# Layer 3 of a four-layer kernel: the weights become the stationary operand, 512 tokens move, and VectorE turns the result

## The chip, the core and the metric

The kernel runs on one core of a Trainium2 chip. The metric is the device time of one execution in microseconds (us), the median of several runs. The engines in this text are TensorE (PE in the profile; PEld is its weight load), VectorE (DVE), ScalarE (ACT), GpSimd (POOL), and SyncE (SP), whose queue issues the DMAs.

## The reference, cut to what matters

```python
def _attn_ref(q, k, v):            # 8 batches, 8 heads, 576 tokens, 64 wide
    q_s = softmax(q, axis=-1); k_s = softmax(k, axis=2)
    kv = np.einsum('bhsd,bhse->bhde', k_s, v)
    return np.einsum('bhsd,bhde->bhse', q_s, kv)
...
x = attn_out.transpose(0, 2, 1, 3).reshape(4608, 512)
h = x @ moe_w_in                   # layer 0: 512 -> 2048
g = np.maximum(0.01 * h, h)
x = g @ moe_w_out                  # layer 1: 2048 -> 512
h = x @ moe2_w_in                  # layer 2: 512 -> 2048
g = h * (1.0 / (1.0 + np.exp(-h)))
return g @ moe2_w_out              # layer 3: 2048 -> 512, the output [4608, 512]
```

The weights arrive as 64-bit floats; the kernel decodes them to 32 bits on ACT and DVE.

## The kernel before, in words

**Precision.** Every fp32 matrix is held as a sum of two float32r parts, high and low, in one tile `[128, 2, 512]`. A product takes three matmuls: high by high, high by low, low by high. ACT copies the high part (line 302), DVE subtracts it from the value to get the low part (line 298).

**Seven products for eight.** Layers 1 to 3 multiply matrices of 2x2 blocks with seven products (c = 1 to 7) in place of eight, with sums of blocks before and sums of products after. The sums of blocks of the weights are made once (`convert`, with a table `PLANS`) and kept in DRAM (`wc`). Of the activations four blocks or sums are kept in DRAM (`gda` for layer 1, `x2d` for layer 2, `gd` for layer 3); three sums more are made on DVE when they are loaded (line 894, `add`).

**Tokens.** 4608 tokens are nine blocks of 512 (`TB`). Layers 1 and 2 go over *supers*: four pairs of blocks and the single last block. Their matmuls have the weights stationary (`lhsT`) and half-blocks of tokens moving: 512 columns for a pair (256 of each block), 256 for the last super. Layer 3 goes over the nine blocks one by one, and there the activations are stationary and the weights move, 256 columns at a time (line 1153): 9 blocks x 4 steps i x 7 products x 12 matmuls = 3024. Its result has tokens in the partitions, so that a finished tile of 512 columns is stored straight from SBUF (`store`, line 1172, 36 stores of 256 KB). Layer 1 in the form of *supers* (line 962) works in two passes over its inner dimension, products 1, 6, 7, 4 (`FIRST`) and then 2, 5, 3 (`SECOND`), with both token halves of a super in PSUM at once: 4 supers x 336 matmuls of 512 columns, and 336 of 256.

**What sets the order.** A planner written in Python (`Queues`) plays all tasks against assumed durations (`v_tt`, `a_`, `pe` and so on for an operation of n columns; 0.73 us for the issue of a DMA of 256 KB and 3 us until it has landed) and ranks, and writes the instructions down in that order. On the chip each engine runs its list strictly in that order, and so does SP's list of DMAs. Operand tiles come from 15 buffers (`g`, `xs`, `xv`, `xr`, `x_108` to `x_115`); a load into one waits until the matmuls that read it are done. 16 tiles `o` of `[128, 512]` hold sums and results. PSUM's eight banks are named `h` and `b`. `a` are weight tiles. Layer 3's weights take the tiles of layer 2's as those come free.

In the code, `layer3` issues the matmuls, `blocks` adds the products of a block up (ACT one copy, DVE eight adds), `store` writes out; `g3_all` loads the operands. `layer1` and `blocks1` are the same for layer 1 (two copies on ACT and six adds on DVE for a token half).

Of the kernel before, what the change touches and what calls it, by code (L numbers as in the profile page):

```python
# [26 lines left out]
def v_tt(n):  # L27
    return 0.16 + n / 960


def v_ts(n):
    return 0.16 + n / 1920


def a_(n):
    return 0.19 + n / 1200


def g_tt(n):
    return 0.15 + n / 430  # L40


def pe(n):
    return 0.007 + n / 2330
# [158 lines left out]
def linear_attention_two_mlps(  # L203
# [62 lines left out]
    gd = [tc.dram_tile([NG, 4, len(s), P, 2, HB], F32, name=f"gd{n}") for n, s in enumerate(supers)]  # L266
# [89 lines left out]
    def split1(f):  # L356
# [336 lines left out]
    def act(j, f, h):  # L693
# [29 lines left out]
    KEPT = (1, 2, 4, 5)  # L723
# [140 lines left out]
    def g1_all():  # L864
        for n in range(NJ):
            pm = merge[n]
            for g, (cs, kind) in enumerate(((FIRST, "b"), (SECOND, ""))):
                for i in range(NG):
                    for q_ in range(2 // pm):
                        at = at1[n, g, i, q_] - 4  # L870
                        yield rank(at)
                        fs = range(4 * i + 2 * q_, 4 * i + 2 * q_ + 2 * pm)
                        yield wait(*(("gd1", j, f) for j in supers[n] for f in fs))
                        src = {
                            c: gd1[n][i, q_ * pm:(q_ + 1) * pm, m].rearrange("z p j n -> p z (j n)")
                            for m, c in enumerate(KEPT1)
                        }
                        yield from operand(
                            [("x", 1, n, g, i, q_)], kind, at, cs, [src], lend, home=HOMES[g]
                        )  # L880

    def g3_all():
        for j in range(NB):
            n, jj = divmod(j, 2)
            for i in range(NG):
                r = at3[j, i] - 4
                yield rank(r)
                yield wait(*(("gd", n, i, rq, c) for c in KEPT for rq in range(2 // merge[n])))
                srcs = {c: gd[n][i, m, jj].rearrange("p r n -> p (r n)") for m, c in enumerate(KEPT)}
                yield from operand([("x", 3, j, i)], "a", r, (1, 5, 2, 6, 4, 7, 3), [srcs], lend)  # L890
# [7 lines left out]
    def blocks(key, r, give):  # L898

        def product(c):  # L900
            yield wait(("p", *key, c))
            return banks[key, c]

        def end(c):
            r_b.put(banks.pop((key, c)))

        p = yield from product(1)
        s = yield get(r_o)
        yield op(("A", a_(TB)))
        copy("A", s, p)  # L910
        end(1)
        p = yield from product(2)
        t = yield get(r_o)
        yield from add(t, s, p)
        end(2)
        spawn(r, give(1, 1, t))
        p = yield from product(6)
        yield from add(s, s, p)
        end(6)
        p = yield from product(7)  # L920
        u = yield get(r_o)
        yield from add(u, s, p)
        end(7)
        p = yield from product(5)
        t = yield get(r_o)
        yield from add(t, u, p)
        spawn(r, give(2, 2, t))
        yield from add(s, s, p)
        end(5)
        p = yield from product(3)  # L930
        yield from add(s, s, p)
        end(3)
        spawn(r, give(1, 2, s))
        p = yield from product(4)
        yield from add(u, u, p)
        end(4)
        spawn(r, give(2, 1, u))

    def layer1():
        for n in range(NJ):  # L940
            w_, pm = width[n], merge[n]
            key = 1, n
            for g, cs in enumerate((FIRST, SECOND)):
                for i, q_ in itertools.product(range(NG), range(2 // pm)):
                    begin, last = not (i or q_), i == NG - 1 and q_ == 2 // pm - 1
                    for c in cs:
                        yield rank(at1[n, g, i, q_])
                        if begin:
                            for mb in range(2 // pm):
                                if c == 2:  # L950
                                    yield wait(("kept", n, mb))
# [3 lines left out]
                        yield wait(("op", ("w", 1, i), c), ("op", ("x", 1, n, g, i, q_), c))  # L955
                        w, x = slot[("w", 1, i), c], slot[("x", 1, n, g, i, q_), c]
# [13 lines left out]
                        if n == NJ - 1 and q_ == 2 // pm - 1:  # L970
                            done(("p", 1, i, c))
                        if last:
                            for mb in range(2 // pm):
                                done(("p", 1, n, mb, c))
                                if c == FIRST[0]:
                                    spawn(-100, blocks1(n, mb))

    def blocks1(n, m):
        key = 1, n

        def product(c):
            yield wait(("p", 1, n, m, c))
# [12 lines left out]
        done(("kept", n, m))  # L995
# [11 lines left out]
        spawn(-100, store1(n, m, 1, 0, t))  # L1007
# [6 lines left out]
        spawn(-100, store1(n, m, 0, 0, t))  # L1014
        p = yield from product(5)
        yield from add(u, u, p)
        spawn(-100, store1(n, m, 1, 1, u))
# [5 lines left out]
        spawn(-100, store1(n, m, 0, 1, s))  # L1023
# [82 lines left out]
    def active(n, i, rq, a, b, t, bank=None):  # L1106
# [6 lines left out]
        if (a, b) == (2, 2):  # L1113
            made["22", n, i, rq] = t
            done(("22", n, i, rq))
            return
        if (a, b) == (1, 2):
            yield wait(("22", n, i, rq))
            t22 = made["22", n, i, rq]
            yield from add(t, t, t22)  # L1120
            spawn(at, keep(n, i, rq, 4, t22))
        yield from keep(n, i, rq, {(1, 1): 1, (2, 1): 2, (1, 2): 5}[a, b], t)

    def keep(n, i, rq, c, t):
        to = gd[n][i, KEPT.index(c)]
        yield op(("D", 0.73))
        nc.sync.dma_start(
            out=to[0] if merge[n] == 2 else to[:, :, rq].rearrange("j p n -> p j n"),
            in_=t.rearrange("p (j n) -> p j n", n=HB),
        )  # L1130
        yield wait()
# [3 lines left out]
    def layer3():  # L1135


        for j in range(NB):
            for i in range(NG):
                for c in ORDER:  # L1140
                    yield rank(at3[j, i])
                    if i == 0:
                        banks[(3, j), c] = yield get(r_b)
                    bank = banks[(3, j), c]
                    yield wait(("op", ("w", 3, i), c), ("op", ("x", 3, j, i), c))
                    x, s = slot[("w", 3, i), c], slot[("x", 3, j, i), c]
                    yield op(("P", 12 * pe(HB)))
                    for m in range(2):
                        for n, (r, a, b) in enumerate(
                            (r, a, b) for r in range(2) for a, b in ((0, 0), (0, 1), (1, 0))  # L1150
                        ):
                            at = r * HB + m * P
                            nc.tensor.matmul(  # L1153
                                bank[:, m * HB:(m + 1) * HB], lhsT=s[:, a, at:at + P],
                                rhs=x[:, b, r * HB:(r + 1) * HB],
                                start=i + m + n == 0, stop=i == NG - 1 and m + n == 6,
                            )
                    r_x.put(s)
                    if i == NG - 1:
                        done(("p", 3, j, c))  # L1160
                        if c == ORDER[0]:
                            spawn(-100, blocks((3, j), -100, lambda a, b, t, j=j: store(j, a, b, t)))

    def layers():
        yield from layer1()
        yield from layer2()
        yield from layer3()

    def store(j, a, b, t):
        o = out[j * TB:(j + 1) * TB, :].rearrange("(p c) e -> p c e", c=4)  # L1170
        yield op(("D", 0.73))
        nc.sync.dma_start(
            out=o[:, 2 * a - 2:2 * a, (b - 1) * HB:b * HB], in_=t.rearrange("p (c e) -> p c e", c=2)
        )
        yield wait()
        r_o.put(t)

    def later():

        yield wait(*(("unit", n) for n in range(len(units))))  # L1180
        r_x.add(*gbuf)
# [23 lines left out]
    for j in range(NB):  # L1205
        for i in range(NG):
            at3[j, i] = t_
            t_ += 2
# [4 lines left out]
    def weight_rank(l, i, c):  # L1213
        if l == 1:
            return at1[0, int(c in SECOND), i, 0] - 8
        return (at2[0, i] if l == 2 else at3[0, i]) - 8

    with tc.manual_schedule():
# [37 lines left out]
        spawn(base[1] - 4, g1_all())  # L1256
        spawn(sum_rank(0, 0), presums())
        spawn(base[2] - 5, x_all())
        spawn(base[3] - 4, g3_all())
# [32 lines left out]
```

## Time and profile before

| | us |
|---|---|
| timed runs (three) | 1574.66, 1574.81, 1577.5; median 1574.81 |
| profiled execution, its own time | 1576.41 |
| profiled execution, span from first to last instruction | 1574.6 |
| PE busy | 1543.8 (98%) |
| DVE busy | 1092.3 (69%) |
| ACT busy | 893.9 (57%) |

Some 1.8 us of the profiled execution's time lie outside its span. Busy times are sums over instructions: where two instructions of an engine overlap in the records, both count. A weight load (PEld) runs beside the matmul ahead of it.

### The profile page before, as it was taken

To read this page: it belongs to the slowest core of one execution; us is meant where nothing else is said; L and a number is where in the kernel's file an instruction comes from. 1 tells how busy PE (TensorE), PEld (TensorE's weight loads), DVE (VectorE), ACT (ScalarE), POOL (GpSimd) and SP (SyncE) were. 2 spreads that over 40 slices of the span, in tenths; PEclk is the share of its full clock that TensorE was granted. 3 is DMA by queue.
4 is the path that set the end of the run, shared out by engine and by line. 5 is a ranking of instruction groups with operands and counts; after the bars stand their busy time and mean duration, and the time that the engine had idled before them with its cause. 6 is when DMAs were issued, how large, how long until landed. Compare 5 with 4: busy or idle time off the path is not lost.

```text
span 1574.6 us, 26644 instructions
## 1 busy us (share of the span) xinstructions
PE 1543.8 (98%) x9088; PEld 1338.1 (85%) x9088; DVE 1092.3 (69%) x2046; ACT 893.9 (57%) x1965; POOL 39.5 (3%) x56
## 2 busy tenths in 40 slices
PE   5899999999999999999999999999999999999999
PEld 3687888888788888888888888888889999999998
DVE  7997656756656989798878643535258777777774
ACT  7779766786445545454548564546467444444442
POOL 2101100000000000000000000000000000000000
PEclk9999999999999999999999999999999999999999
DMA  8876767786679887989899575757378444444442
GB/s 225 264 207 179 236 211 246 230 266 214 216 264 302 260 276 253 301 250 295 253 306 355 199 256 182 239 195 242 110 238 277 129 134 134 135 131 131 135 128 67
DMA packets 291575, 341.26 MB, mean 217 GB/s; under 512 B 62704, under 2 KB 207088, under 8 KB 291440
## 3 DMA queue, kind: packets, MB, share of 16 engines
q1 hardware_dynamic: 291440, 339.56, 68.5%
q8 instruction: 72, 1.18, 0.3%
q14 instruction: 63, 0.52, 0.1%
HBM read 213.65 MB, written 125.83 MB: 216 GB/s over the span
## 4 chain that ended last, share of the span: by engine, by line
PE 94%; DMA 3%; DVE 2%; SPq 1%; ACT 0%; issue 0%; POOL 0%; DVEq 0%; ACTq 0%; POOLq 0%
PE h L1063 12%; PE b L1153 12%; PE h L1153 11%; PE b L962 11%; PE h L962 10%; PE b L1063 9%; PE h L665 8%; PE h L667 8%; PE h L666 8%; PE a L637 2%; PE a L520 1%; DMA a<-wc 1%; PE a L622 1%; DMA rw<-in_moe_w_in_dram 1%; DMA x<-gda 0%; DMA u<-in_k_dram 0%
## 5 line engine op out<-in xcount | busy, mean ns | idle before, releaser
L665 PE MATMUL h<-x,w 128*128 128x512 f32 x576 | 238.1, 413 | 1.8 <-ACT w L302 1.1
L666 PE MATMUL h<-x,w 128*128 128x512 f32 x576 | 225.5, 392 | 2.5 <-DVE x L298 1.3
L667 PE MATMUL h<-x,w 128*128 128x512 f32 x576 | 226.1, 393 | 0.4 <-DVE w L298 0.4
L302 ACT ACTIVATE x<-x 128x512 fp32r<-128x512 f32 x200 | 124.9, 630 | 135.2 <-DMA x<-gd 58.1
L698 ACT ACTIVATE o<-h 128x512 f32<-128x512 f32 x144 | 86.0, 597 | 117.8 <-PE h L667 108.1
L894 DVE TENSOR_TENSOR o<-o,h 128x512 f32<-128x512 f32 x107 | 72.3, 686 | 113.3 <-ACT o L302 60.4
L298 DVE TENSOR_TENSOR x<-x 128x512 fp32r<-128x512 f32 x200 | 132.1, 687 | 20.1 <-ACT x L302 18.3
L894 DVE TENSOR_TENSOR o<-o,b 128x512 f32<-128x512 f32 x118 | 79.5, 686 | 79.4 <-ACT o L302 31.0
L665 PEld LDWEIGHTS h<-x,w 128*128 128x128 f32 x576 | 109.0, 189 | 27.9 <-ACT x L645 1.5
L666 PEld LDWEIGHTS h<-x,w 128*128 128x128 f32 x576 | 109.0, 189 | 25.1 <-DVE x L298 3.4
L667 PEld LDWEIGHTS h<-x,w 128*128 128x128 f32 x576 | 108.5, 188 | 24.4 <-DVE w L298 0.8
L962 PE MATMUL b<-x,a 128*128 128x512 f32 (+1 forms) x498 | 117.6, 374 | 0.4 <-DVE x L298 0.4
L1063 PE MATMUL h<-x,a 128*128 128x512 f32 (+1 forms) x492 | 117.6, 384 | 0.0
L962 PE MATMUL h<-x,a 128*128 128x512 f32 (+1 forms) x510 | 115.0, 364 | 1.9 <-DVE x L298 1.9
L1063 PEld LDWEIGHTS h<-x,a 128*128 128x128 f32 x492 | 90.8, 188 | 18.2
L1153 PE MATMUL h<-a,x 128*128 128x256 f32 x804 | 104.6, 283 | 0.0
L962 PEld LDWEIGHTS b<-x,a 128*128 128x128 f32 x498 | 89.0, 188 | 17.2 <-DVE x L298 0.6
L1153 PE MATMUL b<-a,x 128*128 128x256 f32 x804 | 103.6, 283 | 0.0
L962 PEld LDWEIGHTS h<-x,a 128*128 128x128 f32 x510 | 88.1, 189 | 17.6 <-DVE x L298 2.3
L1153 PEld LDWEIGHTS h<-a,x 128*128 128x128 f32 x804 | 100.1, 192 | 0.0
L1153 PEld LDWEIGHTS b<-a,x 128*128 128x128 f32 x804 | 99.6, 192 | 0.0
L302 ACT ACTIVATE x<-o 128x512 fp32r<-128x512 f32 x119 | 72.9, 626 | 39.3 <-DVE o L894 34.5
(157 smaller groups left out, 2943.5 us busy)
## 6 DMA issues: line engine op xcount, KB each, us to landing
x<-gda SPq DMA_DIRECT2D x152, 256.0 KB, 3.9
gda<-o SPq DMA_DIRECT2D x144, 256.0 KB, 2.7
gd<-o SPq DMA_DIRECT2D x144, 256.0 KB, 2.8
a<-wc SPq DMA_DIRECT2D x84, 256.0 KB, 5.1
x<-gd SPq DMA_DIRECT2D x78, 256.0 KB, 2.7
wc<-o SPq DMA_DIRECT2D x72, 256.0 KB, 3.2
x2d<-o SPq DMA_DIRECT2D x72, 256.0 KB, 4.0
raw<-in_moe_w_out_dram SPq DMA_DIRECT2D x32, 512.0 KB, 5.0
```

What stands on the lines that cost most here:

```text
L298: engines[e].tensor_tensor(out=out_, in0=a, in1=b.bitcast(F32), op=ALU.subtract)
L302: nc.scalar.activation(out=out_, in_=in_, func=ACTF.Copy)
L520: nc.tensor.matmul(pk[o, 0:D + 1], lhsT=kc[:, o], rhs=vv[:, c, h * (D + 1):(h + 1) * (D + 1)], start=c == 0, stop=c == 4,)
L637: nc.tensor.matmul(po, lhsT=kv[bb, p], rhs=qT.rearrange("p (c t) -> p c t", c=4)[:, :, a:e], start=True, stop=True)
L665: nc.tensor.matmul(h, lhsT=w[:, 0, kk], rhs=x[:, 0], start=kk == 0, stop=False)
L666: nc.tensor.matmul(h, lhsT=w[:, 0, kk], rhs=x[:, 1], start=False, stop=False)
L667: nc.tensor.matmul(h, lhsT=w[:, 1, kk], rhs=x[:, 0], start=False, stop=kk == KD - 1)
L698: nc.scalar.activation(out=o, in_=h, func=ACTF.Prelu, alpha=0.01)
L894: nc.vector.tensor_tensor(out=o, in0=a, in1=b, op=alu)
L962: nc.tensor.matmul(banks[key, mb, c][:, mo * w_:(mo + 1) * w_], lhsT=w[:, a, at:at + P], rhs=x[:, b, z * w_:(z + 1) * w_], start=begin and ...
L1063: nc.tensor.matmul(bank[:, z * w_:(z + 1) * w_], lhsT=w4[:, a, rq * pm + z, kc], rhs=x[:, b, ko:ko + w_], start=INTO[c] == c and not (z or ...
L1153: nc.tensor.matmul(bank[:, m * HB:(m + 1) * HB], lhsT=s[:, a, at:at + P], rhs=x[:, b, r * HB:(r + 1) * HB], start=i + m + n == 0, stop=i = ...
```

## The change

Layer 3 takes layer 1's form. `layer1` becomes `wide(l)`, `g1_all` becomes `g_all(l)`, and both serve layers 1 and 3; `layer3`, `blocks`, `keep` and `store` go. The weights are the stationary operand, every second column of a tile's 256 (`p (n m) -> p m n`, m=2), and 512 columns of tokens move. The result then has output features in the partitions, and `out3` turns it: DVE transposes 32x32 squares of 128 columns at a time from four result tiles (two for the last super) into new tiles, and `put3` writes each of those with four DMAs of 64 KB from 32 partitions, in runs of 512 bytes (before: one DMA of 256 KB from 128 partitions, runs of 1 KB). The layout of layer 3's weights changes to fit (`PLANS[3]`, and `load_bits` takes a tile of `moe2_w_out` in two DMAs in place of one, in runs of 512 bytes). `steady()` sets shorter assumed durations for DVE and ACT from attention's end on; for 512 columns on DVE 0.598 us where the planner assumed 0.693, for 256 columns on PE 0.120 where it assumed 0.117.

```diff
+FIXED = {"tt": 0.16, "ts": 0.16, "a": 0.19, "g": 0.15, "pe": 0.007}
+RATE = {"tt": 960, "ts": 1920, "a": 1200, "g": 430, "pe": 2330}
+def steady():
+    FIXED.update(tt=0.065, ts=0.09, a=0.11, pe=0.0133)
+    RATE.update(a=1050, pe=2400)
...
     def load_bits(dst, l, o, f):
+        if l and o:
+            w = w_bits(l, o, f).rearrange("p (a k e) -> p k a e", a=4, k=2)
+            for h in range(2):
+                yield op(("D", 0.73))
+                nc.sync.dma_start(out=dst[:, h * DM:(h + 1) * DM].rearrange("p (a e) -> p a e", a=4), in_=w[:, h])
+            return
...
-        3: ({1: (0, 0), 5: (0, 1), 2: (1, 0), 3: (1, 1)}, "B", (1, 2, 3, 7, 5, 6, 4)),
+        3: ({1: (0, 0), 2: (1, 0), 5: (0, 1), 4: (1, 1)}, "A", (1, 2, 4, 7, 5, 6, 3)),
...
-    def layer1():
+    def wide(l):
+        at_, to = {1: (at1, store1), 3: (at3, store3)}[l]
...
-                                at = (q_ * pm + z) * HB + m * P
+                                at = (q_ * pm + z) * HB
+                                wm = w[:, a, at:at + HB]
+                                wm = (
+                                    wm[:, m * P:m * P + P] if l == 1
+                                    else wm.rearrange("p (n m) -> p m n", m=2)[:, m]
+                                )
                                 nc.tensor.matmul(
-                                    banks[key, mb, c][:, mo * w_:(mo + 1) * w_], lhsT=w[:, a, at:at + P],
+                                    banks[key, mb, c][:, mo * w_:(mo + 1) * w_], lhsT=wm,
                                     rhs=x[:, b, z * w_:(z + 1) * w_],
...
-    def layer3():
-                    yield op(("P", 12 * pe(HB)))
...
-                            nc.tensor.matmul(
-                                bank[:, m * HB:(m + 1) * HB], lhsT=s[:, a, at:at + P],
-                                rhs=x[:, b, r * HB:(r + 1) * HB],
...
+    def out3(n, t):
+        pm, parts = merge[n], [(jj, mm) for jj in range(len(supers[n])) for mm in range(2)]
+        have = [(k, m) for k in (1, 0) for m in range(2 // pm)]
+        last = n == NJ - 1
+        yield rank(-50 if last else at3[n, 1, NG - 1, 0])
+        yield wait(*(("c", n, m, k, t) for k, m in have[:1 if last else 4]))
+        o2 = []
+        for _ in parts:
+            o2.append((yield get(r_o)))
+        for k, m in have:
+            yield wait(("c", n, m, k, t))
+            o = made.pop(("c", n, m, k, t))
+            for q_, (jj, mm) in enumerate(parts):
+                to = o2[q_].rearrange("p (g k c m) -> p k m g c", k=2, c=32, m=2)
+                for z in range(pm):
+                    at = jj * HB + z * width[n] + mm * P
+                    yield op(("V", v_tt(P)))
+                    nc.vector.transpose(
+                        to[:, k, m * pm + z], o[:, at:at + P].rearrange("p (g c) -> p g c", c=32)
+                    )
+            r_o.put(o)
+        for q_, (jj, mm) in enumerate(parts):
+            spawn(-50 if last else at3[n, 1, NG - 1, 0], put3(supers[n][jj], 2 * t + mm, o2[q_]))
+
+    def put3(j, c, o):
+        rows = out[j * TB:(j + 1) * TB, :].rearrange("(g r c) (a e) -> c a r g e", g=4, c=4, a=4)
+        for a in range(4):
+            yield op(("D", 0.25))
+            nc.sync.dma_start(
+                out=rows[c, a], in_=o[32 * a:32 * a + 32].rearrange("r (g e) -> r g e", g=4)
+            )
+        yield wait()
+        r_o.put(o)
```

On PE, at the start of layer 3, the rows were these (destination bank, then moving operand or weights, shape of the moving operand, and how many alike in a row):

```order
L1153 MATMUL b<-a_3720,x_113 128x256 x12
L1153 MATMUL b<-a_4876,x_115 128x256 x12
L1153 MATMUL h<-a_3721,x_108 128x256 x12
L1153 MATMUL h<-a_3722,x_110 128x256 x12
L1153 MATMUL h<-a_4901,x_114 128x256 x12
```

and at the same place there now stand:

```order
L920 MATMUL b<-g,a_3720 128x512 x6
L920 MATMUL h<-g,a_3721 128x512 x6
L920 MATMUL h<-g,a_3722 128x512 x3
L920 MATMUL b<-g,a_3722 128x512 x3
L920 MATMUL b<-xs,a_3723 128x512 x3
L920 MATMUL h<-xs,a_3723 128x512 x3
```

An operand that was used by twelve matmuls of 256 columns is used by six of 512, and the same weight tile returns for the second half of the inner dimension four operands later.

On DVE, where a block of layer 3 ended, the adds of its products (`o<-o,b` and `o<-o,h`) stood between the sums and splits of the next operands:

```order
L894 TENSOR_TENSOR o_153<-o_151,h 128x512
L894 TENSOR_TENSOR o_151<-o_151,h 128x512
L894 TENSOR_TENSOR o_146<-o_151,b 128x512
L894 TENSOR_TENSOR o_145<-x_113,x_112 128x512
L894 TENSOR_TENSOR o_144<-o_146,b 128x512
L894 TENSOR_TENSOR o_151<-o_151,b 128x512
```

Where the first super of layer 3 ends there now stand, from the last adds on:

```order
L887 TENSOR_TENSOR o_143<-o_143,b 128x512
L887 TENSOR_TENSOR o_156<-o_157,xv 128x512
L1113 STREAM_TRANSPOSE o_155<-o_142 128x4x32
L294 TENSOR_TENSOR xv<-xv 128x512
L1113 STREAM_TRANSPOSE o_152<-o_142 128x4x32
L294 TENSOR_TENSOR xr<-o_156,xr 128x512
L887 TENSOR_TENSOR o_156<-xr,o_157 128x512
L1113 STREAM_TRANSPOSE o_147<-o_142 128x4x32
L294 TENSOR_TENSOR x_112<-o_157,x_112 128x512
L1113 STREAM_TRANSPOSE o_148<-o_142 128x4x32
L294 TENSOR_TENSOR xr<-o_156,xr 128x512
L1113 STREAM_TRANSPOSE o_155<-o_151 128x4x32
```

27 more transposes follow without a break, and only then the sums and splits of the operand group `x_113, x_114, x_115, x_108`; the same run of 32 stands at the end of each of the four wide supers.

On SP, the DMAs of the end of the program were:

```order
L740 DMA x_112<-gd_99 128x512
L1172 DMA out_dram<-o_142 128x2x256
L1172 DMA out_dram<-o_151 128x2x256
L1172 DMA out_dram<-o_148 128x2x256
L1172 DMA out_dram<-o_150 128x2x256
```

and are now:

```order
L739 DMA x_115<-gd_99 128x2x256
L739 DMA x_108<-gd_99 128x2x256
L1124 DMA out_dram<-o_143 32x4x128 x4
L1124 DMA out_dram<-o_147 32x4x128 x4
L1124 DMA out_dram<-o_156 32x4x128 x4
L1124 DMA out_dram<-o_145 32x4x128 x4
```

After the end of each of the four wide supers, too, 32 such DMAs stand in one piece between the loads of operands.

## Rows read from the trace of the kernel before

**Rows 1.** The page: span, PE's busy time, granted clock in 40 slices (tenths).

```profile
span 1574.6 us, 26644 instructions
PE 1543.8 (98%) x9088; PEld 1338.1 (85%) x9088; DVE 1092.3 (69%) x2046; ACT 893.9 (57%) x1965; POOL 39.5 (3%) x56
...
PEclk9999999999999999999999999999999999999999
```

**Rows 2.** Busy time of each engine in stretches; the last three are layers 3, 2, 1.

```profile
core 0: us, PE busy (x) PEld busy (x) DVE busy (x) ACT busy (x) POOL busy (x), PEclk, DMA share, GB/s
0.00:100.00 100.00, 78.58 (x442) 57.08 (x443) 86.57 (x202) 73.36 (x198) 17.71 (x37) 0.98 0.84 242
...
800.00:900.00 100.00, 96.04 (x576) 85.49 (x575) 77.28 (x129) 64.51 (x110) 0.00 (x0) 1.00 0.88 295
...
1207.70:1570.90 363.20, 363.17 (x3027) 362.96 (x3025) 260.77 (x415) 157.71 (x256) 0.00 (x0) 1.00 0.43 128
880.00:1060.00 180.00, 180.00 (x796) 149.05 (x795) 84.03 (x132) 93.10 (x161) 0.00 (x0) 1.00 0.64 209
480.00:780.00 300.00, 300.00 (x1325) 248.43 (x1324) 251.26 (x420) 152.95 (x260) 0.00 (x0) 1.00 0.86 272
```

**Rows 3.** PE's waits from 800 to 1210: us in total, times, longest.

```profile
PE h L962 <- DVE x L298: 1.9, 2, 1.4
PE b L1063 <- ACT o L302: 1.7, 2, 1.4
PE h L962 <- DVE g L298: 1.3, 2, 0.8
PE b L962 <- DVE x L298: 0.4, 1, 0.4
PE b L962 <- DVE xs L298: 0.3, 1, 0.3
```

**Rows 4.** The chain that ended last, in time: start, us, matmuls.

```profile
510.28 2.72 PE b L962 x12
...
846.34 2.88 PE h L962 x24
...
873.00 2.72 PE b L1063 x12
...
1207.99 2.88 PE b L1153 x24
```

**Rows 5.** DVE operations by form: count, busy us, mean ns, idle before.

```profile
L298 DVE TENSOR_TENSOR x<-x 128x512 fp32r<-128x512 f32 x200 | 132.1, 687 | 20.1 <-ACT x L302 18.3
...
L481 DVE TENSOR_TENSOR m<-o 128x128 f32<-128x128 f32 x32 | 14.3, 446 | 0.8
...
L298 DVE TENSOR_TENSOR x<-a,x 128x128 fp32r<-128x128 f32 x8 | 2.3, 285 | 1.1 <-ACT x L645 1.1
```

**Rows 6.** DVE's timeline at 1329: start us, us, operation.

```profile
1328.99 0.69 DVE L894 TENSOR_TENSOR o<-o,h 128x512 f32<-128x512 f32 x1
1329.59 0.68 DVE L894 TENSOR_TENSOR o<-x,o 128x512 f32<-128x512 f32 x1
1330.19 0.68 DVE L894 TENSOR_TENSOR o<-xr,o 128x512 f32<-128x512 f32 x1
```

**Rows 7.** DMA issues on SP by line: ns min/median/max; then issue to landing.

```profile
L740 SPq DMA_DIRECT2D x<-gd x78: 319/320/1265, 1156.8 to 1546.4; - x78
...
L1172 SPq DMA_DIRECT2D out_dram<-o x36: 372/388/389, 1241.9 to 1571.6; - x36
...
DMA to landing us min/median/max: 2.1/2.5/4.3
...
L472 SPq DMA_DIRECT2D u<-in_k_dram x32: 596/629/969, 1.2 to 281.8; - x32
```

**Rows 8.** The page, DMA issues: KB each, median us to landing.

```profile
x<-gd SPq DMA_DIRECT2D x78, 256.0 KB, 2.7
```

**Rows 9.** The timeline of the end.

```profile
1569.27 1.60 PE L1153 MATMUL b<-a,x 128*128 128x256 f32 x12
...
1570.90 0.69 DVE L894 TENSOR_TENSOR o<-o,b 128x512 f32<-128x512 f32 x1 [0.75 <-PE b L1153]
```

**Rows 10.** The timeline at layer 3's first matmul.

```profile
1207.71 2.95 PEld L1153 LDWEIGHTS b<-a,x 128*128 128x128 f32 x24
1207.83 3.04 PE L1153 MATMUL b<-a,x 128*128 128x256 f32 x24
```

More of the change, by code (lines that the diff above doesn't have):

```diff
@@ L24, with cost @@
 SLACK = 1.0
[L27 to L44, printed above, removed]
+FIXED = {"tt": 0.16, "ts": 0.16, "a": 0.19, "g": 0.15, "pe": 0.007}
[3 more added lines that the diff above has]
+    RATE.update(a=1050, pe=2400)
+def cost(kind):
+    return lambda n: FIXED[kind] + n / RATE[kind]
+v_tt, v_ts, a_, g_tt, pe = (cost(k) for k in ("tt", "ts", "a", "g", "pe"))
 def rank(r):
@@ L265, in linear_attention_two_mlps @@
     gd1 = [tc.dram_tile([NG, 2, 4, P, len(s), HB], F32, name=f"gda{n}") for n, s in enumerate(supers)]
-    gd = [tc.dram_tile([NG, 4, len(s), P, 2, HB], F32, name=f"gd{n}") for n, s in enumerate(supers)]
+    gd = [tc.dram_tile([NG, 2, 4, P, len(s), HB], F32, name=f"gd{n}") for n, s in enumerate(supers)]
     x2d = [tc.dram_tile([2 // m, 7, P, TB], F32, name=f"x2d{n}") for n, m in enumerate(merge)]
@@ L862, in x_all, with g_all @@
                     spawn(r, operand([("x", 2, n, kq)], "", r, (c,), [{c: x2d[n][kq, c - 1]}], lend))
-    def g1_all():
+    def g_all(l):
+        d, at_ = {1: (gd1, at1), 3: (gd, at3)}[l]
         for n in range(NJ):
@@ L869, in g1_all @@
                     for q_ in range(2 // pm):
-                        at = at1[n, g, i, q_] - 4
+                        at = at_[n, g, i, q_] - 4
                         yield rank(at)
-                        fs = range(4 * i + 2 * q_, 4 * i + 2 * q_ + 2 * pm)
-                        yield wait(*(("gd1", j, f) for j in supers[n] for f in fs))
+                        if l == 1:
+                            fs = range(4 * i + 2 * q_, 4 * i + 2 * q_ + 2 * pm)
+                            yield wait(*(("gd1", j, f) for j in supers[n] for f in fs))
+                        else:
+                            yield wait(*(("gd", n, i, q_, c) for c in KEPT1))
                         src = {
-                            c: gd1[n][i, q_ * pm:(q_ + 1) * pm, m].rearrange("z p j n -> p z (j n)")
+                            c: d[n][i, q_ * pm:(q_ + 1) * pm, m].rearrange("z p j n -> p z (j n)")
                             for m, c in enumerate(KEPT1)
@@ L878, in g1_all @@
                         yield from operand(
-                            [("x", 1, n, g, i, q_)], kind, at, cs, [src], lend, home=HOMES[g]
+                            [("x", l, n, g, i, q_)], kind, at, cs, [src], lend, home=HOMES[g]
                         )
[L882 to L890, printed above, removed]
     def add(o, a, b, alu=ALU.add):
@@ L896, in linear_attention_two_mlps @@
     banks = {}
[L898 to L937, printed above, removed]
-    def layer1():
+    def wide(l):
+        at_, to = {1: (at1, store1), 3: (at3, store3)}[l]
         for n in range(NJ):
             w_, pm = width[n], merge[n]
-            key = 1, n
+            key = l, n
             for g, cs in enumerate((FIRST, SECOND)):
@@ L994, in blocks1 @@
         copy("A", s, p)
-        done(("kept", n, m))
+        done(("kept", l, n, m))
         p = yield from product(6)
@@ L1013, in blocks1 @@
         end(2)
[L1014 removed]
+        spawn(-100, to(n, m, 0, 0, t))
         p = yield from product(5)
         yield from add(u, u, p)
[L1017 removed]
+        spawn(-100, to(n, m, 1, 1, u))
         yield from add(s, s, p)
@@ L1112, in active @@
             r_b.put(bank)
[L1113 to L1116, printed above, removed]
+        key = n, i, rq
+        if (a, b) == (1, 1):
+            made["11", key] = t
+            done(("11", key))
         if (a, b) == (1, 2):
[L1118 to L1122, printed above, removed]
@@ L1124, in keep @@
-    def keep(n, i, rq, c, t):
-        to = gd[n][i, KEPT.index(c)]
+            yield wait(("11", key))
+            yield from add(t, t, made["11", key], ALU.subtract)
+            done(("12", key))
+        c = {(1, 1): 1, (2, 1): 2, (2, 2): 3, (1, 2): 5}[a, b]
+        m, pm = KEPT1.index(c), merge[n]
         yield op(("D", 0.73))
         nc.sync.dma_start(
-            out=to[0] if merge[n] == 2 else to[:, :, rq].rearrange("j p n -> p j n"),
-            in_=t.rearrange("p (j n) -> p j n", n=HB),
+            out=gd[n][i, rq * pm:(rq + 1) * pm, m].rearrange("z p j n -> p z (j n)"),
+            in_=t.rearrange("p (z w) -> p z w", z=pm),
@@ L1130, in keep @@
         )
-        yield wait()
+        yield wait(*([("12", key)] if c == 1 else []))
         r_o.put(t)
         done(("gd", n, i, rq, c))
-    def layer3():
[L1138 to L1146, printed above, removed]
-                    yield op(("P", 12 * pe(HB)))
[L1148 to L1152, printed above, removed]
-                            nc.tensor.matmul(
-                                bank[:, m * HB:(m + 1) * HB], lhsT=s[:, a, at:at + P],
-                                rhs=x[:, b, r * HB:(r + 1) * HB],
[L1156 to L1162, printed above, removed]
@@ new lines, in store3 @@
+    def store3(n, m, k, t, o):
+        made["c", n, m, k, t] = o
+        done(("c", n, m, k, t))
+        if False:
+            yield
+    def out3(n, t):
[21 more added lines that the diff above has]
+            spawn(-50 if last else at3[n, 1, NG - 1, 0], put3(supers[n][jj], 2 * t + mm, o2[q_]))
@@ L1164, in layers @@
+    def put3(j, c, o):
[7 more added lines that the diff above has]
+        r_o.put(o)
     def layers():
-        yield from layer1()
+        yield from wide(1)
         yield from layer2()
-        yield from layer3()
@@ L1169, in store @@
[L1169 to L1176, printed above, removed]
+        yield from wide(3)
     def later():
         yield wait(*(("unit", n) for n in range(len(units))))
+        steady()
         r_x.add(*gbuf)
@@ L1204, in linear_attention_two_mlps @@
     base[3] = t_
[L1205 to L1208, printed above, removed]
+    for n in range(NJ):
+        for g in range(2):
+            for i, q_ in itertools.product(range(NG), range(2 // merge[n])):
+                at3[n, g, i, q_] = t_
+                t_ += (4, 3)[g] * 6 * merge[n] * pe(width[n]) / RANK
     def sum_rank(n, kq):
@@ L1255, in linear_attention_two_mlps @@
                     spawn(weight_rank(l, i, c), weight(l, i, c))
-        spawn(base[1] - 4, g1_all())
+        spawn(base[1] - 4, g_all(1))
         spawn(sum_rank(0, 0), presums())
         spawn(base[2] - 5, x_all())
-        spawn(base[3] - 4, g3_all())
+        spawn(base[3] - 4, g_all(3))
+        for n in range(NJ):
+            for t in range(2):
+                spawn(base[3], out3(n, t))
         spawn(base[1], layers())
```

27 lines of the change are left out of this document (13 added, 14 removed), and 2 rows, old and new, of the table SUMS.

## The prediction

> **What bounds the kernel now.** I read the page's head first: PE is busy 1543.8 of a span of 1574.6 us, and its granted clock is the upper level, 2.4 GHz, in every slice [rows 1]. The table by stretches says where the other 30.8 us are: 21.4 in the first 100 us and 4.0 between 800 and 900; in layer 3, 1207.7 to 1570.9, PE has no gap at all [rows 2]. PE's waits after 800 sum to 5.6 us, all at the two changes of layer [rows 3]. So layer 3 ends when PE has issued its 3024 matmuls. The chain of waits, in order of time, gives their price: 24 matmuls of 256 columns take 2.88 us, 120.0 ns each, in layer 3 and also in the last super of layer 1; 12 of 512 columns take 2.72 us, 226.7 ns each, in layers 1 and 2 [rows 4]. The two prices differ by 106.7 ns for 256 columns more, so that a matmul costs 13.3 ns whatever its width. A 512-column matmul is 13.3 ns cheaper than two of 256.
>
> **PE.** 3024 x 120.0 = 362.9 us leave. 4 x 336 matmuls of 512 columns and 336 of 256 come: 1344 x 226.7 + 336 x 120.0 = 304.6 + 40.3 = 344.9 us. That is 18.0 us less, the first term. The same form already runs at these prices in layer 1, last super included, so I take them as they are.
>
> The Trainium skill (TensorE: Matmul & The Clock Gate, "Back-to-back issue gap") gives an isolated warm matmul N/2.4 + 2.5 ns. By it the estimate would be 3024 x 109.2 = 330.1 against 1344 x 215.8 + 336 x 109.2 = 326.7 us, a gain of 3.4 us that the terms below eat up. This case's rows say 13.3 ns where the page says 2.5, in both layers, and the measurement decides.
>
> **DVE and ACT.** Operands stay 252, with a copy and a subtraction each, and 108 sums. Adds of products go from 72 on DVE to 54, copies on ACT from 9 to 18. New are 144 transposes of 128x128. An operation of 512 columns is recorded with 0.69 us [rows 5] but follows the one ahead after 0.60 us [rows 6], so 0.08 us of a record overlap. The trace holds no transpose. Its nearest row is a subtraction of 128x128, 285 ns [rows 5], less 0.08: 0.20 us. The dearest row of that shape is L481 with a mean of 446 ns [rows 5]; not overlapped at all, 0.45 us. Bounds 0.20 to 0.45; I take 0.22, near the subtraction, since both stream 128 columns of SBUF, with a tenth for the turn. DVE's work in layer 3 is then 414 x 0.60 + 144 x 0.22 = 280 us of 345: not the bound on the whole, but the transposes come in bursts of 32.
>
> So the **end of a wide super** decides. Let T0 be the end of its last matmul. Behind it DVE runs two adds and one sum (T0 + 2.4), then five sums and splits among the first transposes (3.0), 32 transposes, and three sums and a split (2.5) before the operand group `x_113` to `x_108`, the fourth group of the next super, has its first member. PE comes to that after twelve operands of 6 x 226.7 ns, T0 + 16.3. DVE is there at T0 + 7.9 + 32 x 0.22 = 14.9: no stall, with 1.4 us in hand. At 0.20 there are 2.0 in hand, at 0.45 it is 22.3: 6.0 us of stall at each of four boundaries. Break-even is 0.26 us a transpose.
>
> The same burst holds **SP's list**: 32 stores stand ahead of three loads of the sixth group, whose sums PE needs at T0 + 27.2. An issue costs 320 ns for runs of 2 KB, 388 for the stores of before with runs of 1 KB, 629 for `u<-in_k_dram` with runs of 256 bytes [rows 7]. For runs of 512 bytes I take 0.39 (128 runs a DMA, fewer than the 256 of the old store), bounds 0.32 to 0.63. The first turned tile is whole at T0 + 5.4 + 13 x 0.22 = 8.2, the 32 issues end at 20.7, three loads land 3.7 later (0.96 for issue, 2.7 to land [rows 8]), three sums or so and a split take 1.8: T0 + 26.2, 1.0 in hand. At 0.63 it is 33.9: 6.7 us of stall at each of the three boundaries where the next super is wide. Both margins are thin, so I set 1 us for all boundaries together.
>
> **The end of the kernel.** Now the last matmul ends at about 1570.9 (1569.27 + 1.60), one add follows from 1570.90 to 1571.6 [rows 9], one store is issued, 0.39, and lands 2.5 later [rows 7]; the span ends at 1574.6, 3.7 us after PE. In the new list the add is followed by three transposes of the tile before and four of the last; the first output tile is whole five transposes after the add, about 1.8 us after PE, and then eight stores are issued one by one, 0.39 each. The last one starts at 1.8 + 7 x 0.39 = 4.5 and takes the 3.0 us that the last store takes now from 1571.6 to the end: 7.5. That is 3.8 us more (3.2 with issues of 0.32, about 6.7 with issues of 0.63 and transposes of 0.45).
>
> **What I cost at nothing.** The stride of two in the stationary operand: the first load of layer 3 runs 0.12 us ahead of its matmul [rows 10], so a contiguous load takes at most that, and a wide matmul would hide one nearly twice as long. Its cover is gone in the last super, where 336 matmuls last only 120 ns; if the load doubled there, they would cost up to 226.7 ns, 35.9 us more. No row has a strided load. (The Trainium skill, SBUF — State Buffer, "Door 1: The DMA port swizzle", its note on cachelines, lets 16-byte lines with two hits run at full rate; a step of two fp32 gives just two. No run here shows it.) The 16 additional DMAs for `moe2_w_out` lie in layer 1, where PE is without a gap at a DMA share of 0.86 [rows 2]; a late tile would be needed only hundreds of us on. `steady()` reorders DVE, ACT and SP from layer 0 on; PE's own order is the same until layer 2. What it can win back are the 5.6 us of waits, and it could add as many; I take nothing, plus or minus 4.
>
> **Sum.** -18.0 + 1.0 + 3.8 = -13.2 us against the profiled span. The profiled execution's own time is 1576.41, of which 1.8 lie outside the span; that is the same in both kernels. The median of the timed runs is 1574.81: 1561.6, say 1562 us, 0.8% less. A change within 0.2%, 3 us, can hardly be told from none.
>
> **The rivals.**
> *Transposes too slow.* For it: 32 in one run, and no row of their kind. Against: layer 1 in the same form is without PE gaps at 84% DVE [rows 2]. At 0.45 us: 4 x 6.0 = 24 and 2 more at the end, less the 1 already set, 1587, slower. It cancels the gain from 0.36 us a transpose. The Trainium skill (VectorE: DVE Perf Modes, "The three transpose paths") gives 311 ns for 128x128 in bf16; taken as a record, with 0.08 overlapped, the estimate is 0.23 and nothing changes. Chance 0.08, half of it on the slow side of no change.
> *Stores issued too slowly.* For it: small runs cost 0.63 elsewhere [rows 7], and loads stand behind them. Against: those are runs of 256 bytes. At 0.50: 3 x 2.6 and 0.8 at the end, 1570; at 0.63: 3 x 6.7 and 1.7, 1583. It cancels the gain from 0.55. Chance 0.13, a third of it slow.
> *Strided weight loads stall the last super.* Up to +35.9: 1598. It decides from 13 us, 39 ns a matmul. Chance 0.05.
> *The fixed cost does not fall away.* If the price went with columns, 512 would cost 240 and the PE term would vanish: 1574.8 + 4.8 = 1579.6. The chain shows 226.7 in two layers [rows 4]; chance 0.02. The page's 2.5 ns would come close to this.
> *The new order adds waits elsewhere,* in the change to layer 2 or in the narrow last super, as there are in layer 1's [rows 3]: +4 to +12, 1566 to 1574. Chance 0.10.
>
> **The numbers.** The forecast holds 0.62, with its own range of 1558 to 1567. The other cases lie nearly all above it. Up to 1576 I leave out the slow halves and about 0.08 on each side: range 1558 to 1576. Faster by over 0.2% (below 1571.7): 0.62 and the milder parts of the cases, 0.77. Same (to 1578): 0.10. Slower: 0.13.
>
> **What the profile after would show.** Right: layer 3 takes about 346 us with 12 matmuls in 2.72 us in the chain, LDWEIGHTS without change in pitch in the last super (24 in 2.88); PE waits at line 920 of about 1 us in all; transposes following each other by about 0.22 us; stores issued in about 0.39 us; 7 to 8 us from PE's last matmul to the end. Wrong: PE waits for DVE (line 294) some 16 us after a super's end, or for loads some 27 us after it; 336 matmuls of 256 columns taking more than 41 us; or a layer 1 or 2 that is longer than before.

## The result, and the profile after

The changed kernel takes 1583.73 us (median of six runs, 1581.58 to 1589.72), the kernel before 1575.51 in the same comparison: a ratio of 1.0055, with a 95% interval of 1.0038 to 1.0071. It is slower by 0.5%, where 1562 us were forecast.

The profiled execution after took 1581.58 us, its span is 1579.8, 5.2 more than before. The head of its page:

```profile
span 1579.8 us, 24807 instructions
PE 1535.7 (97%) x7744; PEld 1275.0 (81%) x7744; DVE 1112.8 (70%) x2181; ACT 895.9 (57%) x1974; POOL 39.4 (2%) x56
```

Against [rows 1], PE has 8.1 us less to do and is idle for 13 us more. To see where, I cut the span at the first and the last matmul of layer 3:

| us | before | after | difference | forecast |
|---|---|---|---|---|
| up to layer 3's first matmul | 1207.83 | 1203.36 | -4.5 | 0 |
| layer 3, first to last matmul | 363.0 | 368.2 | +5.2 | -17.0 |
| from PE's end to the span's end | 3.7 | 8.2 | +4.5 | +3.8 |
| span | 1574.6 | 1579.8 | +5.2 | -13.2 |

The error lies in layer 3. Its stretches, in the columns of [rows 2], first the whole and then a piece of it:

```profile
1203.40:1571.60 368.20, 357.64 (x1682) 302.27 (x1680) 279.54 (x542) 160.31 (x267) 0.00 (x0) 0.99 0.70 199
...
1476.90:1486.00 9.10, 9.10 (x30) 7.37 (x31) 9.03 (x16) 6.55 (x12) 0.00 (x0) 0.73 0.89 303
```

PE is idle for 10.6 us there, where [rows 2] had no gap. In the short piece PE is busy throughout, and 0.73 is the mean of two levels of the granted clock: 0.50 (1.2 GHz) up to 1481.8, 1.00 (2.4 GHz) from 1482.0 on. PE's timeline from the gap before it (start, us, operation, count; in brackets the idle time before):

```profile
1476.83 1.22 PE L920 MATMUL b<-x,a 128*128 128x512 f32 x2 [3.68 <-DVE x L294]
1477.85 2.77 PE L920 MATMUL h<-x,a 128*128 128x512 f32 x6
1480.41 2.93 PE L920 MATMUL b<-x,a 128*128 128x512 f32 x9
1483.18 1.56 PE L920 MATMUL h<-x,a 128*128 128x512 f32 x6
```

The 17 matmuls from 1476.83 to 1483.18 take 6.35 us, where 233.3 ns each make 3.97: 2.4 us lost. Two causes of the rest follow, each in its view. The chain of waits shows first a piece of layer 1, then a piece of a wide super of layer 3, then of the last super:

```profile
523.75 2.72 PE h L920 x12
...
1498.04 2.80 PE b L920 x12
...
1562.93 2.88 PE h L920 x24
```

Layer 1 and the last super keep the prices of [rows 4], 226.7 and 120.0 ns; the wide matmuls of layer 3 cost 2.80 / 12 = 233.3 ns. That is 6.7 ns more, 1344 times: 9.0 us. The records of the same line in 1210 to 1300 (layer 3) and in 500 to 700 (layer 1), ns min/median/max, differ in the weight load by nearly as much, 5 ns:

```profile
L920 PEld LDWEIGHTS h<-x,a x90: 193/193/193, 1210.1 to 1299.5; 128*128 128x128 f32 x90
...
L920 PEld LDWEIGHTS h<-x,a x240: 187/188/188, 516.7 to 699.9; 128*128 128x128 f32 x120
```

PE's waits in layer 3 (us in total, times, longest):

```profile
PE b L920 <- DVE x L294: 4.0, 2, 3.7
PE h L920 <- DVE x L294: 3.2, 1, 3.2
PE b L920 <- DVE g L294: 2.5, 1, 2.5
PE b L920 <- ACT x L298: 0.8, 1, 0.8
```

10.5 us in five waits. The three long ones come behind the first three supers: 2.45 us until 1312.6, 3.2 until 1394.5, 3.7 until 1476.8. What the first waits for shows in SP's timeline (start, us, operation, count), DVE's, and PE's:

```profile
1288.94 1.72 SPq L739 DMA_DIRECT2D g<-gd  x2
1290.75 15.48 SPq L1124 DMA_DIRECT2D out_dram<-o  x32
1306.34 0.37 SPq L739 DMA_DIRECT2D g<-gd  x1
1306.81 0.38 SPq L739 DMA_DIRECT2D xs<-gd  x1
```

```profile
1288.71 5.52 DVE L1113 STREAM_TRANSPOSE o<-o 128x128 f32<-128x128 f32 x28
...
1309.92 0.69 DVE L887 TENSOR_TENSOR o<-g,xs 128x512 f32<-128x512 f32 x1 [7.05 <-DMA xs<-gd]
```

```profile
1309.05 1.10 PE L920 MATMUL b<-g,a 128*128 128x512 f32 x4
1312.60 0.74 PE L920 MATMUL b<-g,a 128*128 128x512 f32 x2 [2.45 <-DVE g L294]
```

The wait is put down to DVE, but DVE itself had been idle for 7.05 us until the load of `xs` landed, and that load was issued behind 32 stores, 15.48 us, 0.484 each. The transposes are not at fault: 28 in 5.52 us, 0.197 each, done at 1294.2. Behind the second and third super the 32 stores take 16.57 and 16.75 us.

Layer 3 adds up: 344.9 as forecast, +9.0 for the wide matmuls, +10.5 of waits, +2.4 for the clock: 366.8 of 368.2. Most of the rest are the ends of records: a matmul's record lasts 0.16 us beyond the start of the next, and a wait is counted from there, five times and once more at the end.

### The profile page after: what moved, and what is told of

Read it like the earlier page. It is cut to its first block, busy times and chain, and to the rows that moved or that the text cites. A ratio compares the mean times of both kernels' runs of the same rounds, so it can differ in the third digit from the quotient of the medians.

```text
span 1579.8 us, 24807 instructions
## 1 busy us (share of the span) xinstructions
PE 1535.7 (97%) x7744; PEld 1275.0 (81%) x7744; DVE 1112.8 (70%) x2181; ACT 895.9 (57%) x1974; POOL 39.4 (2%) x56
## 4 chain that ended last, share of the span: by engine, by line
PE 88%; DVE 4%; DMA 4%; ACT 2%; SPq 1%; issue 1%; POOL 0%; DVEq 0%; ACTq 0%; POOLq 0%
PE b L920 20%; PE h L920 19%; PE h L1021 11%; PE b L1021 9%; PE h L667 8%; PE h L669 8%; PE h L668 8%; PE a L639 2%; DMA a<-wc 1%; PE a L522 1%; SPq L1124 1%; DMA x<-gd 1%; PE a L624 1%; DVE o L887 1%; DMA rw<-in_moe_w_in_dram 1%
## 5 line engine op out<-in xcount | busy, mean ns | idle before, releaser
L920 PE MATMUL b<-x,a 128*128 128x512 f32 (+1 forms) x966 | 233.6, 377 | 5.8 <-DVE x L294 5.0
L920 PE MATMUL h<-x,a 128*128 128x512 f32 (+1 forms) x894 | 209.1, 370 | 3.2 <-DVE x L294 3.2
L920 PEld LDWEIGHTS b<-x,a 128*128 128x128 f32 x966 | 175.5, 192 | 39.4 <-DVE x L294 6.0
L920 PEld LDWEIGHTS h<-x,a 128*128 128x128 f32 x894 | 158.4, 192 | 31.6 <-DVE x L294 3.6
L298 ACT ACTIVATE x<-x 128x512 fp32r<-128x512 f32 x197 | 121.5, 627 | 103.8 <-DMA x<-gd 45.5
L1021 PE MATMUL b<-x,a 128*128 128x512 f32 (+1 forms) x543 | 111.2, 350 | 1.2 <-ACT o L298 1.1
L887 DVE TENSOR_TENSOR o<-o,b 128x512 f32<-128x512 f32 x112 | 74.9, 683 | 50.5 <-PE b L1021 23.7
L1021 PE MATMUL h<-x,a 128*128 128x512 f32 (+1 forms) x465 | 102.4, 359 | 0.5 <-ACT o L298 0.5
L1021 PEld LDWEIGHTS b<-x,a 128*128 128x128 f32 x543 | 88.7, 189 | 15.1 <-ACT o L298 1.8
L1068 ACT ACTIVATE o<-o 128x512 f32<-128x512 f32 x108 | 67.9, 629 | 47.8 <-DVE o L887 47.4
L1021 PEld LDWEIGHTS h<-x,a 128*128 128x128 f32 x465 | 78.7, 189 | 13.9 <-ACT o L298 0.9
L608 ACT ACTIVATE o<-uq,q 128x64 f32<-128x64 f32 x256 | 85.7, 338 | 5.3 <-DVE q L588 5.0
```

The lines of the kernel that those rows point to most:

```text
L298: nc.scalar.activation(out=out_, in_=in_, func=ACTF.Copy)
L608: nc.scalar.activation(out=x4[:, c, h], in_=q4[:, c, h], func=ACTF.Exp, bias=nq[:, at:at + 1], accum_out=sq[:, to:to + 1],)
L887: nc.vector.tensor_tensor(out=o, in0=a, in1=b, op=alu)
L920: nc.tensor.matmul(banks[key, mb, c][:, mo * w_:(mo + 1) * w_], lhsT=wm, rhs=x[:, b, z * w_:(z + 1) * w_], start=begin and c != 2 and not ...
L1021: nc.tensor.matmul(bank[:, z * w_:(z + 1) * w_], lhsT=w4[:, a, rq * pm + z, kc], rhs=x[:, b, ko:ko + w_], start=INTO[c] == c and not (z or ...
L1068: nc.scalar.activation(out=t, in_=t if bank is None else bank, func=ACTF.Silu)
```

## The experiments

Theories: (A) the strided stationary operand makes wide matmuls dearer; (B) the 32 stores in SP's list delay loads. Rivals: (C) the shorter assumed durations spoiled the order; (D) what delays the loads is not the list but the load on the DMA engines or the transposes. Times beside each other are ratios to the kernel before, taken on the same chip.

**Contiguous weights.** Layer 3 reads 128 neighbouring columns as stationary operand; the output's columns come out in another order, the work is the same.

```diff
-                                wm = (
-                                    wm[:, m * P:m * P + P] if l == 1
-                                    else wm.rearrange("p (n m) -> p m n", m=2)[:, m]
-                                )
+                                wm = wm[:, m * P:m * P + P]
```

> The changed kernel with one edit: layer 3's stationary operand is read in 128 adjacent columns in place of every second of 256, so that output columns come in another order. Theory 1 (the stride makes each wide matmul 6.7 ns longer): 12 wide matmuls of layer 3 take 2.72 us again (226.7 ns each, not 233.3), PE's last matmul ends some 9.0 us earlier (1344 x 6.7 ns), the time falls from 1.0055 to about 0.9995 of the kernel before, or a little less if the waits shift. Rival (the longer pitch comes from something else in layer 3, the transposes or the two banks in turn): the pitch stays at 233.3 ns and the time does not move by more than 2 us. The last super stays at 24 matmuls in 2.88 us by both.

Measured: 1578.4 us, ratio 1.0015 (1.0004 to 1.0025), about 6 us less than after by the ratios, where I expected 9 (the profiled executions differ by 2.7). Its chain, first a wide super of layer 3:

```profile
1497.11 2.72 PE b L917 x12
...
1560.23 2.88 PE h L917 x24
```

The wide matmul is back at 226.7 ns, so the stride did cost 6.7 ns. But not all 9.0 us return: counted from the end of a super, PE comes sooner to loads that come no sooner. Its waits in layer 3:

```profile
PE b L917 <- DVE x L294: 4.9, 2, 4.6
PE h L917 <- DVE x L294: 4.6, 1, 4.6
PE b L917 <- DVE g L294: 3.1, 1, 3.1
```

They sum to 12.6 us (10.5 after), and now the granted clock falls behind each of the three long ones (here after the first two, as means over stretches that hold both levels; columns: stretch, PE busy, clock, DMA share, GB/s):

```profile
1309.00:1330.00 21.00, 19.19 (x78) 0.92 0.85 267
...
1388.00:1412.00 24.00, 19.44 (x74) 0.86 0.84 259
```

78 matmuls at 226.7 ns are 17.7 us, and PE was busy for 19.2; 74 are 16.8, and it was busy for 19.4. With 1.7 behind the third wait, the clock cost some 6 us, where it cost 2.4 in after.

**The stride in layer 1 too.** Layer 1 also takes every second column (its result's columns are mixed by it).

```diff
-                                wm = (
-                                    wm[:, m * P:m * P + P] if l == 1
-                                    else wm.rearrange("p (n m) -> p m n", m=2)[:, m]
-                                )
+                                wm = wm.rearrange("p (n m) -> p m n", m=2)[:, m]
```

> The changed kernel with one edit: layer 1, too, reads its stationary operand with a step of two, so that its result's columns are mixed up. Theory 1 (a step of two costs 6.7 ns at 512 moving columns and nothing at 256, wherever it stands): layer 1's wide matmuls go from 226.7 to 233.3 ns, its four wide supers take 9 us more, its last super is as before with 24 in 2.88 us. Rival (the pitch has to do with layer 3 only): layer 1 stays at 226.7 ns.

Measured: 1591.64 us in one run, 10.1 more than the profiled execution of after. The chain, a wide super of layer 1 and then its last super:

```profile
509.38 2.80 PE b L917 x12
...
824.41 2.88 PE b L917 x24
```

The price appears where the stride is put, at 512 columns and not at 256. Theory A stands.

**Loads first.** The stores behind a super get a later rank, so that loads go between them; the stride stays.

```diff
-            spawn(-50 if last else at3[n, 1, NG - 1, 0], put3(supers[n][jj], 2 * t + mm, o2[q_]))
+            spawn(-50 if last else at3[n + 1, 1, 0, 0], put3(supers[n][jj], 2 * t + mm, o2[q_]))
```

> The changed kernel with one edit: the stores of a wide super get a later rank than the loads of the next super, so that loads stand between the 32 stores in SP's list and not behind them. Transposes stay in one burst of 32. Theory 1 (the waits of 2.5, 3.2 and 3.7 us some 27 us after a super's end are loads held up behind 32 store issues of 0.48 us): these three waits fall below 0.5 us each, the clock stays at its upper level behind them, and the time falls by 9 to 13 us, to 0.997 to 0.9995 of the kernel before. Rival (DVE is late because of its 32 transposes): the three waits stay within a microsecond of what they were, and the time with them.

Measured: 1566.35 us, ratio 0.9939 (0.9924 to 0.9954): faster than both kernels, by about 17 us against after, more than the 9 to 13 that I expected (the profiled executions differ by 15.3). The 28 transposes still run without a break. SP's timeline behind the first super, where no store keeps a load waiting for long:

```profile
1289.69 0.39 SPq L1124 DMA_DIRECT2D out_dram<-o  x1
1290.71 0.32 SPq L739 DMA_DIRECT2D g<-gd  x1
1291.08 1.39 SPq L1124 DMA_DIRECT2D out_dram<-o  x3
1292.57 0.41 SPq L739 DMA_DIRECT2D xs<-gd  x1
```

and layer 3 as a whole (columns of [rows 2]):

```profile
1202.30:1556.30 354.00, 354.00 (x1682) 299.67 (x1680) 280.06 (x543) 160.41 (x267) 0.00 (x0) 1.00 0.73 207
```

No gap and the full clock: 354.0 us, which is 344.9 + 9.0. The stores' place cost 368.2 - 354.0 = 14.2 us, theory B's share.

**Stores from GpSimd's queue.** The stores keep their old rank, but go from another queue than the loads.

```diff
-            yield op(("D", 0.25))
-            nc.sync.dma_start(
+            yield op(("G", 0.25))
+            nc.gpsimd.dma_start(
```

> The changed kernel with all output stores issued from GpSimd's queue, ranks as they were. Theory 1 (loads are late because they stand behind the stores' issues in SP's list): the waits at the supers' ends go below 1 us each though the same stores run on the same DMA engines at the same time; about 10 us less than the changed kernel unless the end gets longer. Rival (the stores' runs of 512 bytes keep the DMA engines from the loads): the waits stay above 2 us.

Measured: 1569.5 us in one run, the kernel before 1576.91. An issue there takes 548 ns, longer than on SP, and yet layer 3 has no gap:

```profile
1202.50:1556.50 354.00, 354.00 (x1682) 299.64 (x1680) 281.70 (x543) 162.03 (x267) 70.81 (x131) 1.00 0.72 207
```

As many bytes and transposes, none of the waits: rival D falls. It is the list that loads and stores share. The end got longer, as the expectation allowed for: 11.2 us from PE's last matmul in place of 8.2, with 16 issues in 8.66 us.

**The kernel before with the shorter durations alone.**

```diff
+FIXED = {"tt": 0.16, "ts": 0.16, "a": 0.19, "g": 0.15, "pe": 0.007}
...
         yield wait(*(("unit", n) for n in range(len(units))))
+        steady()
```

(The functions of the durations, cut here, are those of the changed kernel.)

> The kernel before with only the shorter assumed durations from attention's end on. In the changed kernel layer 3 begins 4.5 us earlier than before. Theory (that is the shorter durations, which move splits ahead at the change to layer 2): the waits between 800 and 1210 fall from 5.6 us to about 2, layer 3 begins at about 1203.5 and the time is 0.9965 to 0.998 of the kernel before. Rival (it is the new plan of layer 3's weights and operands, not the durations): the time is within 0.1% of the kernel before.

Measured: 1570.5 us, ratio 0.9968 (0.9956 to 0.9981), a gain of 4.9 us. Of [rows 3], 5.6 us in eight waits, 1.8 in four are left:

```profile
PE b L1059 <- ACT o L298: 1.3, 2, 0.9
PE h L1059 <- ACT o L298: 0.5, 2, 0.3
```

All waits of line 962 are gone. They lay in layer 1's last super, at 821 to 843, and layer 2 now begins at 854.2 in place of 860.6.

**After without the shorter durations.**

```diff
-        steady()
```

> The changed kernel without the shorter assumed durations: layer 3's new form alone. By theory 1 the form costs in this order of the lists: wide matmuls at 233.3 ns (+9.0 us against the forecast), three waits of 2 to 5 us behind the 32 stores, and a longer end; the shorter durations alone brought 4.9 us to the kernel before. So 1588 us, 1.0075 to 1.0095 of the kernel before, if the two parts add up. Rival (the shorter durations make the lists too tight for layer 3, and without them the waits at the supers' ends go): the three waits fall below 1 us and the time is at or below that of the changed kernel.

Measured: 1594.08 us, ratio 1.0114 (1.0095 to 1.0133), 9 to 10 us more than after and more than I expected. Layer 3 starts at 1203.34, as early as in after, but takes 378.1 us. Its longest waits are others than those of after:

```profile
PE b L920 <- ACT x L298: 4.5, 2, 2.7
PE h L920 <- ACT g L298: 4.5, 1, 4.5
PE b L920 <- ACT xv L298: 2.4, 1, 2.4
```

All waits there sum to 13.7 us, and near each of the three long ones the granted clock falls (means of 0.66 to 0.89 in stretches of 10 us). So `steady()` helps, and rival C falls. It is worth 4.9 us with the old form and about twice that with the new one. In the old form its gain lies before layer 3 (which starts at 1202.1 in place of 1207.8); the new one starts layer 3 as early without it, for a reason that no run singles out, and there the gain lies in layer 3. Parts of this change cannot simply be added.

**Both repairs.** Loads first, and layer 3's weights laid out in SBUF so that the 128 columns wanted lie side by side: `moe2_w_out` comes in four DMAs a tile, in runs of 256 bytes, and `out3` places its columns to match.

```diff
-            w = w_bits(l, o, f).rearrange("p (a k e) -> p k a e", a=4, k=2)
-            for h in range(2):
+            w = w_bits(l, o, f).rearrange("p (a k m e) -> p k m a e", a=4, k=2, m=2)
+            for h in range(4):
...
+                                wm = wm[:, m * P:m * P + P]
...
-                to = o2[q_].rearrange("p (g k c m) -> p k m g c", k=2, c=32, m=2)
+                to = o2[q_].rearrange("p (g k m c) -> p k m g c", k=2, c=32, m=2)
...
+            spawn(-50 if last else at3[n + 1, 1, 0, 0], put3(supers[n][jj], 2 * t + mm, o2[q_]))
```

> The changed kernel with both costs taken away: stationary operand in adjacent columns, the order of output columns kept right by loading moe2_w_out in four DMAs a tile with runs of 256 bytes in place of two with 512, and loads ahead of stores in SP's list. Theory 1: wide matmuls of layer 3 at 226.7 ns, no wait over 1.2 us at the ends of supers; 9 us less than with loads first alone (0.9939), so about 1557.5 us, 0.988 to 0.9895. Rival (the shorter matmuls only turn into waits for operands, DVE or SP): not below 0.992.

Measured: 1560.15 us, ratio 0.9903 (0.9884 to 0.9921), a little above what I expected. It beats both kernels: about 1% against before. Layer 3 takes 348.0 us. Its waits:

```profile
PE b L919 <- DVE o L889: 1.2, 2, 1.0
PE h L919 <- DVE o L889: 0.4, 1, 0.4
```

1.6 us, new, behind sums on DVE. The contiguous weights bring 6.0 of their 9.0 us here.

**Two queues at the end.** As the last, but of the last super's stores every second goes from ACT's queue.

```diff
+            act = j == NB - 1 and a % 2
...
-            nc.sync.dma_start(
+            (nc.scalar if act else nc.sync).dma_start(
```

> The kernel of e10 with half of the last super's stores issued from ScalarE's queue. Theory (from PE's last matmul to the end it is eight store issues of 0.48 us on one queue): the end comes after about 6.5 us in place of 8.2, and the time falls by 1 to 2 us against e10. Rival (the end waits for the landing of the last store and the transposes, not for issues): no change.

Measured: 1559.68 us, ratio 0.99 (0.988 to 0.9919). It is 0.5 us less than without, inside both intervals: inconclusive. In the profiled executions the end takes 7.6 us in place of 8.2, where 6.5 were expected: eight issues on each of two queues take 6.3 us, sixteen on one took 7.6. What else holds the end stays open.

## Why the prediction was wrong, by its own steps

**The step that failed first: "What I cost at nothing. The stride of two in the stationary operand."** I took its price to be hidden by a wide matmul and looked for harm only in the last super, as a rival of up to 35.9 us. It was the other way round: the last super pays nothing, each wide matmul pays 6.7 ns, 9.0 us in all. That the load starts 0.12 us ahead of its matmul [rows 10] bounds neither its length nor its effect, and the trace of before had the length (ns min/median/max):

```profile
L1153 PEld LDWEIGHTS b<-a,x x804: 192/192/192, 1207.7 to 1570.5; 128*128 128x128 f32 x161
```

A contiguous load is recorded with 192 ns, not with 120 at most, and still a matmul starts every 120. The chain had already shown, at 13.3 ns for every matmul, that something besides the columns is paid each time; I gave that price no cause and did not ask whether a longer load raises it. The prediction's sentence on the Trainium skill (SBUF — State Buffer, "Door 1: The DMA port swizzle", its note on cachelines) let a step of two fp32 run at full rate; in the weight load of a wide matmul these runs show 193 ns against 188 and a pace of 233.3 against 226.7. Why 256 columns do not pay stays open: there, too, the record of the load is longer, 195 against 192 ns, but the pace stays 120.0.

**The step that failed most: the stores in SP's list, set at 0.39 each, with 1.0 us in hand and 1 us for all boundaries.** Its mechanism and its place were right: the rival "stores issued too slowly" had waits of 2.6 us at 0.50, and 2.45, 3.2 and 3.7 came at 0.484 to 0.523. Behind the first super, whose 336 matmuls run from 1203.4 to T0 = 1281.8, the steps went thus:

| us after T0 | forecast | measured |
|---|---|---|
| first store issued | 8.2 | 9.0 |
| 32 issued | 20.7 | 24.4 |
| load landed, DVE begins | 24.4 | 28.1 |
| operand ready | 26.2 | 30.7 |
| PE asks for it | 27.2 | 28.4 |

The stores account for 2.9 of the 4.5 us between forecast and measured. I had set the old store's 388 ns, the length of an issue alone; the new issue's median is 438, and some 45 more pass before the next. A margin of 1.0 us was smaller than what a tenth of a microsecond in the price, 3.2 us over 32 issues, could take. The row for 256 bytes [rows 7] already gave 0.63, and the value should have been put between the two.

**What the rival left out: the clock, and the last super.** The list's place cost 14.2 us in place of the 7.8 that 0.50 gave. The three long waits make 9.4 of it, and 1.1 are two waits in the last super, which are gone with loads first. In the third long wait the granted clock fell to 1.2 GHz, which cost 2.4 us more, so a wait cost more than its length; the ends of records make up most of the rest. The runs of after lie 8.1 us apart, those with loads first 1.5; the granted clock over a run was 0.945 to 0.996 in the one and 0.997 to 0.999 in the other. The clock alone does not order them (the run at 0.945 took 1584.9 us, the longest, 1589.72, had 0.992), so what spreads them stays open.

**`steady()`, "nothing, plus or minus 4".** Alone it wins 4.9 us, nearly all of the 5.6 us that I named as what it could win back; the term should have been a gain, not nothing.

**What held.** The price of 226.7 and 120.0 ns wherever weights are contiguous. Of the term of -18.0 the kernel with both repairs reaches 15.0: it runs layer 3 in 348.0 us, 3.1 above the 344.9, and 1.6 of these are waits. The transposes: 0.197 us each against 0.22 taken, and DVE ready with `x_113` in time. The end: +4.5 against +3.8. And the start of layer 3 came 4.5 us earlier, a gain that I had not counted. Either part of the change brings it alone, `steady()` in the old form and the new form without `steady()`, and the two do not add.

Together: 9.0 for the stride, 13.2 for the boundaries (14.2 against 1.0) and 0.7 at the end, less 4.5 ahead of layer 3, are 18.4 us, the distance between -13.2 and +5.2.

## What to carry to other kernels

A new access pattern of a stationary operand is to be priced at every width it is used with, not only where the matmul looks too short to hide it: a few nanoseconds on each of 1344 matmuls were half of the 18.0 us that the new form was to save. Stores that stand ahead of loads in one DMA list hold the loads back by their number times the pace of the issues (here 32 times 0.484 us and more); put them between the loads or on another queue, and compare any margin with what the uncertainty of one price does over the whole burst. A repair upstream of a late load gives little until the load itself is earlier: contiguous weights were back at full pace at once, but part of their gain turned into longer waits and lost clock.

## What the runs showed of the hardware that I had not expected

- Stationary fp32r operands read with a step of two: a matmul of 512 columns every 233.3 ns in place of 226.7, one of 256 columns every 120.0 either way.
- A store of 64 KB from 32 partitions in runs of 512 bytes takes SP as long to issue as, or longer than, a store of 256 KB from 128 partitions in runs of 1 KB: median 438 ns against 388 [rows 7]. On GpSimd it is 548.
- In a gap of 3.7 us on PE the granted clock fell to 0.50 (1.2 GHz), and it was 0.50 from 1475.2 to 1481.8, while matmuls ran again from 1476.8. After gaps of 2.5 and 3.2 us in the same execution it was 1.00 (2.4 GHz) in the next 9 us; with contiguous weights gaps of 3.1 and 4.6 us went with such a fall.
